# Heads paired as h and h+4, and keys dealt nine tokens to a row

## The chip, the cores and the metric

The kernel runs on one core of a Trainium2 chip. The metric is the device time of one execution in microseconds (us); the kernel before has a median of 513.19 us in three runs (512.69 to 513.75). The core has a matrix engine (TensorE, PE in the profile, with PEld for its weight loads), a vector engine (VectorE, DVE), an activation engine (ScalarE, ACT), a general engine (GpSimd, POOL) and an engine that mostly starts transfers (SyncE, SP). Each takes its instructions in the order in which the program gives them, and they wait for each other by semaphores.

## The reference

```python
q, k, v: (8, 8, 576, 64) float32            # batch, heads, tokens, head_dim
scores = q @ k.T / 8                        # 576 x 576 for each of 64 heads
thresh = max(scores, row) - tau             # tau = 0.02
attn   = softmax(where(scores >= thresh, scores, -1e9))
x      = (attn @ v), heads side by side     # (4608, 512)
h      = x @ w_in                           # (4608, 2048)
g      = h * clip(h + 3, 0, 6) / 6
out    = g @ w_out                          # (4608, 512)
```

The order of the heads in x is free as long as the rows of w_in are taken in the same order, and the order of the keys of a head is free as long as the rows of v are taken in the same order.

## The kernel before

Two heads are a pair, two pairs a quad: 16 quads, two for each of the 8 batches. The heads of a pair lie in partitions 0 to 63 and 64 to 127 of the transposed tiles `qT` and `kT` (head_dim on the partitions, tokens along them), so that two score matmuls work in the two halves of the array. A pair has 4 tiles of 128 query rows and one rest of 64; the rests of both pairs of a quad share a tile. So a quad has 9 slots, and 144 slots n = 0 to 143 follow each other in one written-out loop (`for n, sl in enumerate(queue)`). Everything around it is placed by n: the dictionaries `turns` (transposes of q and k of a later quad), `products` (attention times v), and the lists `loads`, `vcasts`, `casts`, of which `start` takes transfers at the end of a slot. There is no scheduler: the order in the text is the order on each engine.

For slot n, two heads: `scores(n)` (L295, PE), `sm_max` (L310, DVE: copy out of PSUM with the row maximum), `sm_bias` (L317, POOL), `sm_mask` (L322, ACT), `sm_exp` (L327, ACT, with the row sum), `sm_recip` (L330, DVE), `sm_norm` (L335, POOL, writes `pn` in bfloat16). `pn` is transposed by a DMA on SP's queue (L343) or, early on, by PE (L350). `av_main` and `av_rest` (L359, L362) multiply with v; DVE copies the result into `xT` or `xR` (L370, L380).

From slot 22 on (`N1`), each slot also does a piece of the second half: `mm1` (L394 or L389), eight matmuls of x with w_in into PSUM bank `HB`; `mm1_relu` (ACT in even slots, L402; DVE in odd slots, L404); `mm1_gate` (L417, DVE), which frees the bank; and in even slots two parts of `mm2` (L428, 8 matmuls with w_out), copied out every second even slot by DVE (`osb`, L436). Scores are issued by two slots at once at the end of each odd slot. So from about 107 us on, two slots make one round of PE work: L295 (16 matmuls; 24 when one of the slots is the rest of a quad), L394 (even slot), L428, L394 (odd slot), L359 and L362. In such a round DVE does, in this order: copy of `xT`; relu and gate of the odd slot; a transpose of q or k, where `turns` has one; two maxima; gate of the even slot; two maxima; every second round the copy of `osb`.

How q and k get into `qT` and `kT`:

- Batches 0 and 1 (`b < NB`, `by_pe`): loaded in 128 rows, transposed by PE against an identity (L236) and copied out of PSUM. The last 64 tokens of the four heads of a quad come in a tile `kr` (k) and in the end of `nq` (q), as two transfers of 32 KB each (L127), and go through one PE transpose each (L261, L263).
- Batches 2 to 7 (quads 4 to 15): loaded in 32 by 32 blocks, so that VectorE's block transpose from SBUF to SBUF (L245 for q with 576 columns, L251 for k with 512) gives `qT` and `kT` without PE. A pair of q is loaded by four transfers of 72 KB (`blocks_q`), the first 512 keys of a pair by four of 64 KB (`blocks_k`). k is dealt four tokens to a row. The last 64 keys still take the old way: transfers of `kr` (L127; on SP's queue for quad 4, on POOL's from quad 5 on), a PE transpose (L261) in an even slot six or five before the quad, and at the start of the next slot two copies out of PSUM into the two halves of `kT` (`copy_out`, L226, ACT from slot 24 on), columns 576 to 639 for the lower head and 0 to 63 for the upper. `kT` has 640 columns for that reason, and `scores` begins at column 64 for the lower head.

v comes in bfloat16 through POOL's queue (`load_v`, L144 and L147): for batches from 2 on, four transfers for the first 512 tokens, two heads each over 128 partitions, and two for the last 64. w_in comes in 16 transfers of 128 partitions by 512 columns (L165), taken from `casts` in slots 4 to 15, with two in slots 5, 8, 11 and 14.

PSUM has 8 banks. Banks 2 and 5 are handed out in turn by `bank()`, to the PE transposes and to the products with v.

Of the kernel before, what the change touches and what calls it, by code (L numbers as in the profile page):

```python
# [9 lines left out]
F32 = mybir.dt.float32  # L10
# [5 lines left out]
P = 128  # L16
# [4 lines left out]
def kernel(  # L21
# [10 lines left out]
    nc = tc.nc  # L32
# [49 lines left out]

    def load_quad(quad):
        b, g = divmod(quad, 2)
        nat[quad] = (nat_pool.tile([P, 1152], F32, tag="nq", name="nq"),
                     nat_pool.tile([P, 4, 4, D], F32, tag="km", name="km"),
                     nat_pool.tile([P, 2 * D], F32, tag="kr", name="kr"))
        nq, km, kr = nat[quad]

        def main(dst, src, h, order, by=nc.sync):  # L90
            by.dma_start(out=dst[:, :, h, :], in_=src[b, 4 * g + h, 0:512, :].rearrange(order, t=4))

        def blocks_q(n, a, j):
            c = 32 * (2 * a + j)
            nc.sync.dma_start(out=nq[c:c + 32, n * S:(n + 1) * S].rearrange("p (k d) -> p k d", d=32),
                              in_=q[b, 4 * g + 2 * n + a, :, 32 * j:32 * j + 32].rearrange("(k r) d -> r k d", r=32))

        def blocks_k(n, a, j):
            c = 32 * (2 * a + j)
            nc.sync.dma_start(  # L100
                out=km[c:c + 32].rearrange("p t h d -> p (t h d)")[:, n * 512:(n + 1) * 512].rearrange(
                    "p (t m d) -> p t m d", t=4, d=32),
                in_=k[b, 4 * g + 2 * n + a, 0:512, 32 * j:32 * j + 32].rearrange("(m r t) d -> r t m d", r=32, t=4))

        def load_k(n):
            if b < NB:
                for a in range(2):
                    main(km, k, 2 * n + a, "(p t) d -> p t d", by=nc.scalar if quad == n == 0 else nc.sync)
            else:
                for a in range(2):  # L110
                    for j in range(2):
                        blocks_k(n, a, j)

        def load_q(n):
            if b < NB:
                for a in range(2):
                    main(nq[:, 0:1024].rearrange("p (t h d) -> p t h d", h=4, t=4), q, 2 * n + a, "(t p) d -> p t d")
            else:
                for a in range(2):
                    for j in range(2):  # L120
                        blocks_q(n, a, j)

        def rest():
            for dst, src in ((kr[:], k), (nq[:, 1024:1152], q))[0:2 if b < NB else 1]:
                for n in range(2):
                    by = nc.scalar if quad == 0 and src is k else nc.sync if quad < 5 else nc.gpsimd
                    by.dma_start(out=dst[64 * n:64 * n + 64, :].rearrange("p (h d) -> p h d", h=2),  # L127
                                 in_=src[b, 4 * g + 2 * n:4 * g + 2 * n + 2, 512:S, :].rearrange("h p d -> p h d"))

        def both():  # L130
            rest()
            load_k(1)

        if b < NB:
            loads.extend((lambda: load_k(0), lambda: load_q(0), rest, lambda: load_k(1), lambda: load_q(1)))
        else:
            loads.extend((lambda: load_q(0), lambda: load_k(0), lambda: load_q(1), both))

    def load_v(b):
        vm = v_pool.tile([P, H, 4 * D], BF16, tag="vm", name="vm")  # L140
        vr = vrs[b % 2]
        vsb[b] = (vm, vr)
        w = 4 if b < NB else 2
        mains = [lambda h=h: nc.gpsimd.dma_start(  # L144
            out=vm[:, h:h + w, :], in_=v[b, h:h + w, 0:512, :].rearrange("h (p t) d -> p h (t d)", t=4))
            for h in range(0, H, w)]
        rests = [lambda a=a: nc.gpsimd.dma_start(  # L147
            out=vr[a * 64:(a + 1) * 64, a, :, :],
            in_=v[b, :, 512:S, :].rearrange("(hp a) p d -> a p hp d", a=2)[a]) for a in range(2)]
        vcasts.extend(mains + rests if b < NB else mains[0:1] + rests + mains[1:])  # L150


    vrs = []
# [6 lines left out]
    w_out_sb = singles.tile([P, NI, d_model], BF16)  # L160

    def load_weights():
        for n4 in range(4):
            for ki in range(KI):
                casts.append(lambda n4=n4, ki=ki: nc.gpsimd.dma_start(  # L165
                    out=w_in_sb[:, ki, n4 * 512:(n4 + 1) * 512],
                    in_=moe_w_in[ki * P:(ki + 1) * P, n4 * 512:(n4 + 1) * 512]))
        for ni in range(NI):
            casts.append(lambda ni=ni: nc.gpsimd.dma_start(
                out=w_out_sb[:, ni, :], in_=moe_w_out[ni * P:(ni + 1) * P, :]))  # L170
# [39 lines left out]
    def kT_of(pair):  # L210
        return qkT[pair // 2][1][:, pair % 2, :]
# [17 lines left out]
    def by_pe(pair):  # L229
        return pair // NPAIR < NB  # L230
# [16 lines left out]
    def transpose_k(pair):  # L247
        if not by_pe(pair):
            n = pair % 2
            km = nat[pair // 2][1][:].rearrange("p t h d -> p (t h d)")  # L250
            nc.vector.transpose(out=kT_of(pair)[:, 64:576], in_=km[:, n * 512:(n + 1) * 512])  # L251
            return None
        pb = main_pe(nat[pair // 2][1], pair)
        return lambda: copy_out(kT_of(pair)[:, 64:576], pb)

    def transpose_rest(quad, of_k=True, of_q=True):
        pb = bank()
        nq, _, kr = nat[quad]
        of_q = of_q and by_pe(2 * quad)
        if of_k:  # L260
            nc.tensor.transpose(pb[:, 0:P], kr[:], identf[:])  # L261
        if of_q:
            nc.tensor.transpose(pb[:, P:2 * P], nq[:, 1024:1152], identf[:])  # L263

        def evict():
            qT, kT = qkT[quad]
            both = pb.rearrange("p (w n t) -> p w n t", n=2, t=64)
            if of_q:
                nc.vector.tensor_copy(out=qT[:, :, 512:S], in_=both[:, 1])
            if of_k:  # L270
                copy_out(kT[0:64, :, S:S + 64], both[0:64, 0])
                copy_out(kT[64:P, :, 0:64], both[64:P, 0])
        return evict
# [9 lines left out]
    def scores(n):  # L283
        quad, slot = divmod(n, NSLOT)
        w0 = 320 if first(n) else 384
        parts = ((0, w0), (w0, S - w0))
        heads = range(2)
        for group in [((a,), parts) for a in heads] if n in (1, 2) else [(heads, (part,)) for part in parts]:
            for i in range(2 if slot == 8 else 1):
                for a, (k0, w) in [(a, part) for part in group[1] for a in group[0]]:  # L290
                    pair = 2 * quad + (i if slot == 8 else slot // 4)
                    rows = slice(64 * i, 64 * i + 64) if slot == 8 else slice(0, P)
                    q0 = 512 if slot == 8 else slot % 4 * P
                    c0, kc = score_col(n, a) + k0, 64 * (1 - a) + k0
                    nc.tensor.matmul(ps_flat[rows, c0:c0 + w],  # L295
                                     qT_of(pair)[a * 64:(a + 1) * 64, q0:q0 + rows.stop - rows.start],
                                     kT_of(pair)[a * 64:(a + 1) * 64, kc:kc + w], start=True, stop=True)
# [56 lines left out]
    def av(pb, pair, pT, cols):  # L354
        b, hp = divmod(pair, NPAIR)
        vm, vr = vsb[b]
        for c in range(4):
            for a in range(2):
                nc.tensor.matmul(pb[a * 64:(a + 1) * 64, :], vm[:, 2 * hp + a, c * D:(c + 1) * D],  # L359
                                 pT[:, 5 * a + c, cols], start=(c == 0), stop=False)  # L360
        for a in range(2):
            nc.tensor.matmul(pb[a * 64:(a + 1) * 64, :], vr[:, a, hp, :], pT[:, 4, cols], start=False, stop=True)  # L362
# [136 lines left out]
    for quad in range(1, NQUAD):  # L499
        n0 = quad * NSLOT  # L500
        first_odd = n0 - 9 + quad % 2
        for i, (job, of) in enumerate((("q", 2 * quad), ("k", 2 * quad), ("rest", quad),
                                       ("q", 2 * quad + 1), ("k", 2 * quad + 1))):
            turn_at(n0 + ((-5, -5, -4, -2, -1) if quad == 1 else (-6, -5, -4, -2, -1))[i] if quad < 3 else
                    first_odd + (0, 2, 3, 4, 6)[i] if quad > 3 else first_odd + (0, 2, 3, 5, 7)[i], job, of)

# [32 lines left out]
    for n, sl in enumerate(queue):  # L539
# [111 lines left out]
        elif n not in (4, 12, 15, 18, 21) and not 23 < n < 30 and (n < 37 or n % 2 == 0):  # L651
            start(loads, 1)
        if n < 4 or 15 < n < 20 or n > 33:
            start(vcasts, 1 if n < N1 or n % 2 else 0)
        else:
            start(casts, 2 if n in (5, 8, 11, 14) or 21 < n < 28 else 1)
        prev = sl
# [87 lines left out]
```

## Time and profile before

| | |
|---|---|
| three runs, median (us) | 513.19 |
| the profiled execution: first to last instruction (us) | 511.0 |
| what lies around it, by the median of the runs (us) | 2.2 |
| PE, DVE, ACT, POOL busy | 99, 87, 88, 58% |
| granted PE clock | 0.999 |
| L261, transposes of kr by PE | 15, 274 ns |
| L226, copies of the last keys by ACT | 24, 253 ns |
| L245, block transposes 128x576 by DVE | 24, 771 ns |
| L251, block transposes 128x512 by DVE | 24, 704 ns |
| L127, transfers of kr issued by POOL | 22, 632 ns |
| L165, transfers of w_in issued by POOL | 16, 569 ns |

The profile is of one execution, and gives of its own time only the span of 511.0 us; the runs are 1.5 to 2.7 us longer than that, which holds what lies before the first and behind the last instruction. A busy share says how much of the span some instruction of the engine was under way. Matmuls overlap, so the rate at which PE works is read from the distance between the starts of its groups, not from their lengths: a PE transpose is under way for 274 ns, but the next matmul starts 0.11 us after it.

### The profile page before, as it was taken

To read this page: it belongs to the slowest core of one execution; us is meant where nothing else is said; L and a number is where in the kernel's file an instruction comes from. 1 tells how busy PE (TensorE), PEld (TensorE's weight loads), DVE (VectorE), ACT (ScalarE), POOL (GpSimd) and SP (SyncE) were. 2 spreads that over 40 slices of the span, in tenths; PEclk is the share of its full clock that TensorE was granted. 3 is DMA by queue.
4 is the path that set the end of the run, shared out by engine and by line. 5 is a ranking of instruction groups with operands and counts; after the bars stand their busy time and mean duration, and the time that the engine had idled before them with its cause. 6 is when DMAs were issued, how large, how long until landed. Compare 5 with 4: busy or idle time off the path is not lost.

```text
span 511.0 us, 12107 instructions
## 1 busy us (share of the span) xinstructions
PE 503.4 (99%) x4132; PEld 319.8 (63%) x4132; DVE 442.8 (87%) x1127; ACT 450.3 (88%) x977; POOL 298.6 (58%) x539
## 2 busy tenths in 40 slices
PE   8999999999999999999999999999999999999997
PEld 7656566666655666666655666666655666667564
DVE  4788899989999999999999999999999999887251
ACT  4999999999999999999999999999999999987160
POOL 2788879666666756656565656666566755552000
PEclk9999999999999999999999999999999999999999
DMA  6998999989999999999899999999999996563132
GB/s 144 182 172 147 153 143 182 174 157 178 188 160 172 163 174 160 205 162 181 150 158 181 154 163 163 179 169 175 163 178 149 187 177 116 114 111 75 72 57 77
DMA packets 314318, 78.77 MB, mean 154 GB/s; under 512 B 296880, under 2 KB 309424, under 8 KB 314256
## 3 DMA queue, kind: packets, MB, share of 16 engines
q1 hardware_dynamic: 294464, 67.90, 78.0%
q0 software_dynamic: 18304, 9.64, 15.6%
q8 instruction: 32, 0.52, 0.4%
q10 hardware_dynamic: 1488, 0.46, 0.4%
q14 instruction: 30, 0.25, 0.2%
HBM read 36.70 MB, written 9.44 MB: 90 GB/s over the span
## 4 chain that ended last, share of the span: by engine, by line
PE 80%; DVE 4%; ACT 3%; issue 1%; DVEq 0%
PE ps L295 24%; PE ps L428 23%; PE ps L394 20%; PE ps L359 7%; PE ps L389 3%; DVE s L310 1%; PE ps L362 1%; ACT s L327 1%; ACT s L322 1%; DVE g L417 1%; DVE r L404 1%; PE ps L668 1%; ACT r L402 1%; PE ps L350 0%; DVE xT L370 0%
## 5 line engine op out<-in xcount | busy, mean ns | idle before, releaser
L335 POOL TENSOR_SCALAR pn<-s,rinv 128x576 bf16<-128x576 f32 x288 | 210.6, 743 | 19.4 <-issue 4.8
L310 DVE TENSOR_SCALAR_CACHE_REDUCE s<-ps 128x576 f32<-128x576 f32 x288 | 205.0, 748 | 13.4 <-POOL pn L335 5.1
L322 ACT ACTIVATE s<-s,bias 128x576 f32<-128x576 f32 x288 | 205.7, 762 | 3.6 <-POOL bias L317 3.2
L327 ACT ACTIVATE s<-s 128x576 f32<-128x576 f32 x288 | 192.5, 671 | 0.3
L295 PE MATMUL ps<-kT,qT 64*128 64x384 f32 (+7 forms) x1280 | 175.5, 419 | 2.1 <-DVE s L310 2.0
L295 PEld LDWEIGHTS ps<-kT,qT 64*128 64x128 f32 (+1 forms) x1280 | 103.7, 175 | 57.8 <-issue 15.6
L394 PE MATMUL ps<-xT,w_in_sb 128*128 128x256 bf16 x1024 | 131.0, 273 | 0.6 <-DVE g L417 0.5
L428 PE MATMUL ps<-w_out_sb,g 128*128 128x512 bf16 x560 | 130.7, 379 | 0.0
L394 PEld LDWEIGHTS <-w_in_sb 128*128 128x128 bf16 x1024 | 95.6, 98 | 40.3 <-issue 21.0
L317 POOL TENSOR_SCALAR bias<-m 128x2 f32<-128x2 f32 (+1 forms) x147 | 27.5, 187 | 148.4 <-DVE rinv L330 132.1
L417 DVE SCALAR_TENSOR_TENSOR g<-r,ps 128x512 bf16<-128x512 f32 x128 | 87.8, 687 | 13.6 <-ACT r L402 9.1
L428 PEld LDWEIGHTS <-g 128*128 128x128 bf16 x560 | 54.6, 98 | 55.0 <-issue 0.4
L402 ACT ACTIVATE r<-ps,three 128x512 f32<-128x512 f32 x81 | 55.4, 686 | 25.1 <-PE ps L394 20.2
L327 ACT ACTIVATION_READ_ACCUMULATOR s<-s 128x1 f32 x288 | 54.5, 189 | 0.0
L404 DVE TENSOR_SCALAR r<-ps 128x512 f32<-128x512 f32 x63 | 42.9, 681 | 0.0
L359 PE MATMUL ps<-pT,vm 128*64 128x256 bf16 (+1 forms) x480 | 39.1, 285 | 0.0
L359 PEld LDWEIGHTS <-vm 128*64 128x64 bf16 x736 | 27.2, 110 | 16.1 <-issue 14.7
L370 DVE CAST xT<-ps 128x256 bf16<-128x256 f32 (+1 forms) x60 | 26.2, 437 | 10.2 <-PE ps L362 10.2
L436 DVE TENSOR_SCALAR osb<-ps 128x512 f32<-128x512 f32 x31 | 20.8, 672 | 8.4 <-PE ps L428 8.4
L310 DVE DVE_READ_ACCUMULATOR s<-ps 128x1 f32 x288 | 23.9, 83 | 0.0
L330 DVE RECIPROCAL rinv<-rsum 128x2 f32<-128x2 f32 x144 | 23.0, 160 | 0.7 <-ACT s L327 0.6
L144 POOL DMA_DIRECT2D vm<-in_v_dram x28 | 21.4, 766 | 0.1
(60 smaller groups left out, 256.6 us busy)
## 6 DMA issues: line engine op xcount, KB each, us to landing
out_dram<-osb SPq DMA_DIRECT2D x31, 256.0 KB, 2.6
nq<-in_q_dram SPq DMA_DIRECT2D x96, 72.0 KB, 3.4
km<-in_k_dram SPq DMA_DIRECT2D x96, 64.0 KB, 3.2
vm<-in_v_dram POOLq DMA_DIRECT2D x24, 128.0 KB, 3.9
nq<-in_q_dram SPq DMA_DIRECT2D x16, 128.0 KB, 4.9
w_in_sb<-in_moe_w_in_dram POOLq DMA_DIRECT2D x16, 128.0 KB, 3.7
w_out_sb<-in_moe_w_out_dram POOLq DMA_DIRECT2D x16, 128.0 KB, 4.1
pT<-pn SPq DMA_TRANSPOSE x117, 3.8
```

Of the source, the lines that this page charges most:

```text
L295: nc.tensor.matmul(ps_flat[rows, c0:c0 + w], qT_of(pair)[a * 64:(a + 1) * 64, q0:q0 + rows.stop - rows.start], kT_of(pair)[a * 64:(a + 1) ...
L310: nc.vector.tensor_scalar(out=sl.s[:, i, :], in0=ps_flat[:, c0:c0 + S], scalar1=1.0, scalar2=None, op0=Alu.mult, op1=Alu.max, accum_out=sl ...
L317: nc.gpsimd.tensor_scalar(out=sl.bias[:, of], in0=sl.m[:, of], scalar1=-scale, scalar2=tau, op0=Alu.mult, op1=Alu.add)
L322: nc.scalar.activation(out=s, in_=s, func=Act.Prelu, bias=sl.bias[:, i:i + 1], scale=scale, alpha=REJECT)
L327: nc.scalar.activation(out=s, in_=s, func=Act.Exp, accum_out=sl.rsum[:, i:i + 1])
L335: nc.gpsimd.tensor_scalar(out=pn[:, i, :], in0=sl.s[:, i, :], scalar1=sl.rinv[:, i:i + 1], scalar2=1.0, op0=Alu.mult, op1=Alu.mult)
L359: nc.tensor.matmul(pb[a * 64:(a + 1) * 64, :], vm[:, 2 * hp + a, c * D:(c + 1) * D], pT[:, 5 * a + c, cols], start=(c == 0), stop=False)
L394: nc.tensor.matmul(ps[:, hb, n * 256:(n + 1) * 256], w_in_sb[:, ki, (ni + n) * P:(ni + n + 1) * P], xT[b][:, ki, c0:c0 + 256], start=(ki = ...
L402: nc.scalar.activation(out=r, in_=hps, func=Act.Relu, bias=three[:])
L404: nc.vector.tensor_scalar(out=r, in0=hps, scalar1=3.0, scalar2=0.0, op0=Alu.add, op1=Alu.max)
L417: nc.vector.scalar_tensor_tensor(out=out, in0=r, scalar=6.0, in1=hps, op0=Alu.min, op1=Alu.mult)
L428: nc.tensor.matmul(o_ps[0], gbuf[:, ni, mt * P:(mt + 1) * P], w_out_sb[:, ni, :], start=(ni == 0), stop=(ni == NI - 1))
```

## The change

Heads h and h+4 make a pair in place of 2h and 2h+1: pair (g, n) of a batch has heads 2g+n and 4+2g+n. The heads of a quad's two pairs, 2g and 2g+1 below and 4+2g and 5+2g above, now lie next to each other in memory, so one transfer brings both for one half of the partitions (`blocks`): two transfers of 144 KB in place of four of 72 KB (q) or 64 KB (k). For k, rows are dealt nine tokens each in place of four, which takes in all 576 keys. `kr` is no longer loaded for quads 4 to 15, and the turn of their `rest` is left out: no PE transpose and no copies. VectorE transposes 576 columns of k for a pair, by two instructions of 320 and 256 columns, each in runs of 64 columns with steps of 128 between them, on both sides. In `kT` both heads now begin at column 0.

v follows: a head's rows are dealt nine tokens each, in four transfers over 64 partitions with four heads each, and two for the tokens that are left. For batch 2 a transfer is started in each slot from 34 to 39 (before, in odd slots alone). w_in's rows are taken in the new order, in 8 transfers over 64 partitions, four pieces of 512 columns each, in place of 16 over 128 partitions, one piece each; empty places in `casts` keep the rest of the list where it was.

```diff
@@ -82,72 +82,72 @@
 
     def load_quad(quad):
         b, g = divmod(quad, 2)
-        nat[quad] = (nat_pool.tile([P, 1152], F32, tag="nq", name="nq"),
-                     nat_pool.tile([P, 4, 4, D], F32, tag="km", name="km"),
-                     nat_pool.tile([P, 2 * D], F32, tag="kr", name="kr"))
+        nat[quad] = (nat_pool.tile([P, 2 * S], F32, tag="nq", name="nq"),
+                     nat_pool.tile([P, 2 * S], F32, tag="km", name="km"),
+                     nat_pool.tile([P, 2 * D], F32, tag="kr", name="kr") if b < NB else None)
         nq, km, kr = nat[quad]
 
-        def main(dst, src, h, order, by=nc.sync):
-            by.dma_start(out=dst[:, :, h, :], in_=src[b, 4 * g + h, 0:512, :].rearrange(order, t=4))
-
-        def blocks_q(n, a, j):
-            c = 32 * (2 * a + j)
-            nc.sync.dma_start(out=nq[c:c + 32, n * S:(n + 1) * S].rearrange("p (k d) -> p k d", d=32),
-                              in_=q[b, 4 * g + 2 * n + a, :, 32 * j:32 * j + 32].rearrange("(k r) d -> r k d", r=32))
-
-        def blocks_k(n, a, j):
-            c = 32 * (2 * a + j)
-            nc.sync.dma_start(
-                out=km[c:c + 32].rearrange("p t h d -> p (t h d)")[:, n * 512:(n + 1) * 512].rearrange(
-                    "p (t m d) -> p t m d", t=4, d=32),
-                in_=k[b, 4 * g + 2 * n + a, 0:512, 32 * j:32 * j + 32].rearrange("(m r t) d -> r t m d", r=32, t=4))
+        def main(dst, src, n, a, order, by=nc.sync):
+            by.dma_start(out=dst[:, 0:1024].rearrange("p (t h d) -> p t h d", h=4, t=4)[:, :, 2 * n + a, :],
+                         in_=src[b, 4 * a + 2 * g + n, 0:512, :].rearrange(order, t=4))
+
+        def blocks(dst, src, a, order, **sizes):
+            rows = src[b, 4 * a + 2 * g:4 * a + 2 * g + 2].rearrange("n t d -> (n t) d")
+            for j in range(2):
+                c = 32 * (2 * a + j)
+                nc.sync.dma_start(out=dst[c:c + 32].rearrange("p (k d) -> p k d", d=32) if len(sizes) == 1 else
+                                  dst[c:c + 32].rearrange("p (t x d) -> p t x d", d=32, t=9),
+                                  in_=rows[:, 32 * j:32 * j + 32].rearrange(order, **sizes))
 
         def load_k(n):
             if b < NB:
                 for a in range(2):
-                    main(km, k, 2 * n + a, "(p t) d -> p t d", by=nc.scalar if quad == n == 0 else nc.sync)
+                    main(km, k, n, a, "(p t) d -> p t d", by=nc.scalar if quad == n == 0 else nc.sync)
             else:
-                for a in range(2):
-                    for j in range(2):
-                        blocks_k(n, a, j)
+                blocks(km, k, n, "(x r t) d -> r t x d", r=32, t=9)
 
         def load_q(n):
             if b < NB:
                 for a in range(2):
-                    main(nq[:, 0:1024].rearrange("p (t h d) -> p t h d", h=4, t=4), q, 2 * n + a, "(t p) d -> p t d")
+                    main(nq, q, n, a, "(t p) d -> p t d")
             else:
-                for a in range(2):
-                    for j in range(2):
-                        blocks_q(n, a, j)
+                blocks(nq, q, n, "(k r) d -> r k d", r=32)
 
         def rest():
-            for dst, src in ((kr[:], k), (nq[:, 1024:1152], q))[0:2 if b < NB else 1]:
+            for dst, src in ((kr[:], k), (nq[:, 1024:1152], q)):
                 for n in range(2):
-                    by = nc.scalar if quad == 0 and src is k else nc.sync if quad < 5 else nc.gpsimd
+                    by = nc.scalar if quad == 0 and src is k else nc.sync
                     by.dma_start(out=dst[64 * n:64 * n + 64, :].rearrange("p (h d) -> p h d", h=2),
-                                 in_=src[b, 4 * g + 2 * n:4 * g + 2 * n + 2, 512:S, :].rearrange("h p d -> p h d"))
-
-        def both():
-            rest()
-            load_k(1)
+                                 in_=src[b].rearrange("(a n) t d -> n a t d", a=2)[2 * g + n, :, 512:S, :].rearrange(
+                                     "a p d -> p a d"))
 
         if b < NB:
             loads.extend((lambda: load_k(0), lambda: load_q(0), rest, lambda: load_k(1), lambda: load_q(1)))
         else:
-            loads.extend((lambda: load_q(0), lambda: load_k(0), lambda: load_q(1), both))
+            loads.extend((lambda: load_q(0), lambda: load_k(0), lambda: load_q(1), lambda: load_k(1)))
 
     def load_v(b):
         vm = v_pool.tile([P, H, 4 * D], BF16, tag="vm", name="vm")
         vr = vrs[b % 2]
         vsb[b] = (vm, vr)
-        w = 4 if b < NB else 2
-        mains = [lambda h=h: nc.gpsimd.dma_start(
-            out=vm[:, h:h + w, :], in_=v[b, h:h + w, 0:512, :].rearrange("h (p t) d -> p h (t d)", t=4))
-            for h in range(0, H, w)]
-        rests = [lambda a=a: nc.gpsimd.dma_start(
-            out=vr[a * 64:(a + 1) * 64, a, :, :],
-            in_=v[b, :, 512:S, :].rearrange("(hp a) p d -> a p hp d", a=2)[a]) for a in range(2)]
-        vcasts.extend(mains + rests if b < NB else mains[0:1] + rests + mains[1:])
+        if b < NB:
+            mains = [lambda h=h: nc.gpsimd.dma_start(
+                out=vm[:, h:h + 4, :], in_=v[b, h:h + 4, 0:512, :].rearrange("h (p t) d -> p h (t d)", t=4))
+                for h in range(0, H, 4)]
+            rests = [lambda a=a: nc.gpsimd.dma_start(
+                out=vr[a * 64:(a + 1) * 64, a, :, :],
+                in_=v[b, 4 * a:4 * a + 4, 512:S, :].rearrange("h p d -> p h d")) for a in range(2)]
+        else:
+            def tokens(a, first, count):
+                return v[b, 4 * a:4 * a + 4].rearrange("h (p t) d -> p h (t d)", t=9)[
+                    :, :, first * D:(first + count) * D]
+
+            mains = [lambda a=a, u=u, first=first: nc.gpsimd.dma_start(
+                out=vm[64 * u:64 * u + 64, 4 * a:4 * a + 4, :], in_=tokens(a, first, 4))
+                for a, u, first in ((0, 0, 0), (0, 1, 5), (1, 0, 5), (1, 1, 1))]
+            rests = [lambda a=a: nc.gpsimd.dma_start(
+                out=vr[a * 64:(a + 1) * 64, a, :, :], in_=tokens(a, 4 * (1 - a), 1)) for a in range(2)]
+        vcasts.extend(mains + rests)
 
 
     vrs = []
@@ -160,11 +160,13 @@
     w_out_sb = singles.tile([P, NI, d_model], BF16)
 
     def load_weights():
+        rows = moe_w_in.rearrange("(a ki d) f -> a d ki f", a=2, ki=KI)
         for n4 in range(4):
-            for ki in range(KI):
-                casts.append(lambda n4=n4, ki=ki: nc.gpsimd.dma_start(
-                    out=w_in_sb[:, ki, n4 * 512:(n4 + 1) * 512],
-                    in_=moe_w_in[ki * P:(ki + 1) * P, n4 * 512:(n4 + 1) * 512]))
+            for a in range(2):
+                casts.append(lambda n4=n4, a=a: nc.gpsimd.dma_start(
+                    out=w_in_sb[64 * a:64 * a + 64, :, n4 * 512:(n4 + 1) * 512],
+                    in_=rows[a, :, :, n4 * 512:(n4 + 1) * 512]))
+                casts.append(lambda: None)
         for ni in range(NI):
             casts.append(lambda ni=ni: nc.gpsimd.dma_start(
                 out=w_out_sb[:, ni, :], in_=moe_w_out[ni * P:(ni + 1) * P, :]))
@@ -247,16 +249,19 @@
     def transpose_k(pair):
         if not by_pe(pair):
             n = pair % 2
-            km = nat[pair // 2][1][:].rearrange("p t h d -> p (t h d)")
-            nc.vector.transpose(out=kT_of(pair)[:, 64:576], in_=km[:, n * 512:(n + 1) * 512])
+            rows = nat[pair // 2][1][:].rearrange("p (t n w) -> p t n w", t=9, n=2)[:, :, n, :]
+            out = kT_of(pair)
+            for u in range(2):
+                e = 5 - u
+                nc.vector.transpose(out=out[:, 0:640].rearrange("p (c u w) -> p c u w", u=2, w=64)[:, 0:e, u, :],
+                                    in_=rows[:, 5 * u:5 * u + e, :])
             return None
-        pb = main_pe(nat[pair // 2][1], pair)
+        pb = main_pe(nat[pair // 2][1][:, 0:1024].rearrange("p (t h d) -> p t h d", h=4, t=4), pair)
         return lambda: copy_out(kT_of(pair)[:, 64:576], pb)
 
     def transpose_rest(quad, of_k=True, of_q=True):
         pb = bank()
         nq, _, kr = nat[quad]
-        of_q = of_q and by_pe(2 * quad)
         if of_k:
             nc.tensor.transpose(pb[:, 0:P], kr[:], identf[:])
         if of_q:
@@ -291,7 +296,7 @@
                     pair = 2 * quad + (i if slot == 8 else slot // 4)
                     rows = slice(64 * i, 64 * i + 64) if slot == 8 else slice(0, P)
                     q0 = 512 if slot == 8 else slot % 4 * P
-                    c0, kc = score_col(n, a) + k0, 64 * (1 - a) + k0
+                    c0, kc = score_col(n, a) + k0, (64 * (1 - a) if by_pe(pair) else 0) + k0
                     nc.tensor.matmul(ps_flat[rows, c0:c0 + w],
                                      qT_of(pair)[a * 64:(a + 1) * 64, q0:q0 + rows.stop - rows.start],
                                      kT_of(pair)[a * 64:(a + 1) * 64, kc:kc + w], start=True, stop=True)
@@ -356,7 +361,7 @@
         vm, vr = vsb[b]
         for c in range(4):
             for a in range(2):
-                nc.tensor.matmul(pb[a * 64:(a + 1) * 64, :], vm[:, 2 * hp + a, c * D:(c + 1) * D],
+                nc.tensor.matmul(pb[a * 64:(a + 1) * 64, :], vm[:, 4 * a + hp, c * D:(c + 1) * D],
                                  pT[:, 5 * a + c, cols], start=(c == 0), stop=False)
         for a in range(2):
             nc.tensor.matmul(pb[a * 64:(a + 1) * 64, :], vr[:, a, hp, :], pT[:, 4, cols], start=False, stop=True)
@@ -501,6 +506,8 @@
         first_odd = n0 - 9 + quad % 2
         for i, (job, of) in enumerate((("q", 2 * quad), ("k", 2 * quad), ("rest", quad),
                                        ("q", 2 * quad + 1), ("k", 2 * quad + 1))):
+            if job == "rest" and quad // 2 >= NB:
+                continue
             turn_at(n0 + ((-5, -5, -4, -2, -1) if quad == 1 else (-6, -5, -4, -2, -1))[i] if quad < 3 else
                     first_odd + (0, 2, 3, 4, 6)[i] if quad > 3 else first_odd + (0, 2, 3, 5, 7)[i], job, of)
 
@@ -651,7 +658,7 @@
         elif n not in (4, 12, 15, 18, 21) and not 23 < n < 30 and (n < 37 or n % 2 == 0):
             start(loads, 1)
         if n < 4 or 15 < n < 20 or n > 33:
-            start(vcasts, 1 if n < N1 or n % 2 else 0)
+            start(vcasts, 1 if n < 40 or n % 2 else 0)
         else:
             start(casts, 2 if n in (5, 8, 11, 14) or 21 < n < 28 else 1)
         prev = sl
```

## The prediction

> **What bounds the kernel now.** I read the page first (span, shares, chain), then the stretches of 20 us, then PE's order of time in the steady part, and last DVE and ACT in the same stretch. The page:
>
> ```profile
> span 511.0 us, 12107 instructions
> PE 503.4 (99%) x4132; PEld 319.8 (63%) x4132; DVE 442.8 (87%) x1127; ACT 450.3 (88%) x977; POOL 298.6 (58%) x539
> PE 80%; DVE 4%; ACT 3%; issue 1%; DVEq 0%
> L245 DVE STREAM_TRANSPOSE qT<-nq 128x576 f32<-128x576 f32 x24 | 18.5, 771 | 0.0
> L251 DVE STREAM_TRANSPOSE kT<-km 128x512 f32<-128x512 f32 x24 | 16.9, 704 | 0.0
> ```
>
> (The last two are from the groups kept apart by shape.) PE carries 80% of the chain that ends last, and from 107 us to 500 us the stretches show it busy without a gap. A busy PE is no proof, so PE's order of time in one part of the steady state (start, length, line, count):
>
> ```profile
> 302.73 1.89 PE L428 MATMUL ps<-w_out_sb,g 128*128 128x512 bf16 x8
> 304.45 0.27 PE L261 MATMUL ps<-identf,kr 128*128 128x128 f32 x1
> 304.56 1.04 PE L394 MATMUL ps<-xT,w_in_sb 128*128 128x256 bf16 x8
> ...
> 308.27 1.05 PE L394 MATMUL ps<-xT,w_in_sb 128*128 128x256 bf16 x8
> 309.15 1.89 PE L428 MATMUL ps<-w_out_sb,g 128*128 128x512 bf16 x8
> 310.98 1.03 PE L394 MATMUL ps<-xT,w_in_sb 128*128 128x256 bf16 x8
> ...
> 315.64 1.89 PE L428 MATMUL ps<-w_out_sb,g 128*128 128x512 bf16 x8
> 317.36 1.04 PE L394 MATMUL ps<-xT,w_in_sb 128*128 128x256 bf16 x8
> ```
>
> From L428 to the next group PE needs 1.72 us (315.64 to 317.36) where it does not wait. The transpose of kr takes 0.11 us of it (304.45 to 304.56), far less than its length of 0.27. In the round after, 309.15 to 310.98 is 1.83: a wait of 0.11, of which the busy share shows nothing. Why is seen on ACT and DVE there:
>
> ```profile
> 306.18 0.51 ACT L226 COPY kT<-ps 64x128 f32<-64x128 f32 x2
> 309.52 0.69 ACT L402 ACTIVATE r<-ps,three 128x512 f32<-128x512 f32 x1
> 310.24 0.69 DVE L417 SCALAR_TENSOR_TENSOR g<-r,ps 128x512 bf16<-128x512 f32 x1 [0.26 <-ACT r L402]
> ```
>
> The two copies of the last keys put ACT 0.5 us back, so its relu (L402) comes late, DVE's gate (L417) waits 0.26 for it and ends at 310.93, and the bank is free for L394 0.05 later. So PE is bound by its own issue, and any wait on the even slot's gate is lost for good. How near DVE is to making it wait, in the round from 299.70:
>
> ```profile
> 299.88 0.42 DVE L370 CAST xT<-ps 128x256 bf16<-128x256 f32 x1
> 300.21 0.68 DVE L404 TENSOR_SCALAR r<-ps 128x512 f32<-128x512 f32 x1
> 300.93 0.69 DVE L417 SCALAR_TENSOR_TENSOR g<-r,ps 128x512 bf16<-128x512 f32 x1
> 301.54 0.70 DVE L251 STREAM_TRANSPOSE kT<-km 128x512 f32<-128x512 f32 x1
> 302.16 0.72 DVE L310 TENSOR_SCALAR_CACHE_REDUCE s<-ps 128x576 f32<-128x576 f32 x1
> ...
> 303.65 0.69 DVE L417 SCALAR_TENSOR_TENSOR g<-r,ps 128x512 bf16<-128x512 f32 x1
> ```
>
> The k transpose lies ahead of the even gate. That gate ends at 304.34; with 0.05 behind it, L394 could start at 304.39, and without kr's transpose PE is ready at 304.45.
>
> **The change, part by part.** (1) *PE transposes of kr, 12 removed.* The first (96.60) lies in a wait of PE for the gate, so it gives nothing; 11 others at 0.11: **1.21 us gained**.
>
> (2) *ACT copies, 24 removed.* The wait that follows them is 0.10 to 0.11 in the six rounds that start at 131.3, 189.5, 247.8, 306.0, 364.2 and 422.4 (0.60); where the copies fall in a round with two products (from 157.2, 215.4, 273.7, 331.9, 390.1) L428 to the next takes 1.76 in place of 1.73, five times 0.03 (0.15); and at 98.98 they lie on the chain itself, and L428 (101.86) to L394 (103.80) takes 1.94, so 0.21. The other copies delay nothing. Together **0.96 gained**. Next to be late there is the relu, which then waits for L394 itself (0.31 to 0.38 in the rounds without copies).
>
> (3) *DVE's k transposes, 24 of 512 columns become 24 pairs of 320 and 256.* The rows for 512 and 576 columns, 704 and 771 ns, give 1.05 ns a column and 0.17 us fixed: 0.50 and 0.44 us. The next instruction starts 0.08 before a transpose ends (301.54 + 0.70 against 302.16). So from start to start 0.42 + 0.36 = 0.78 in place of 0.62: 0.16 more each. The steps between runs of 64 are not in the trace for this operation; the nearest row is a copy into two runs of 64 with a step (L269, 283 ns) against one into 128 columns in a row (L478, 292 ns): no price. Bounds: below, only the 64 more columns, 0.07. Above, if each of the nine runs cost a start of its own, 9 x (0.067 + 0.087) = 1.39 less 0.62, so 0.77. In between, if the second waits for the first's end, 0.50 + 0.44 less 0.08 less 0.62, so 0.24; for that speaks L224, whose second copy into the same tile begins only when the first has ended (75.65; the copy before it, over all partitions, overlaps by 0.08). I take 0.16, since the transposes use all 128 partitions as those that overlap do.
>
> What it costs PE: room is what is left before the even gate makes L394 wait. In the round above DVE is ready for the gate at 303.57 (0.08 into L330, which starts at 303.49), and the gate could start at 304.45 - 0.05 - 0.69 = 303.71: room 0.14. This holds in 8 rounds, those that follow a copy of osb. In 9 others `xT` starts 0.07 earlier in the round, room 0.20; in 6 rounds with 24 score matmuls L394 is due 0.16 later, so 0.36; the first (94.22) lies where DVE waits 0.13 for ACT anyway. So with an addition K the loss is 8(K-0.14) + 9(K-0.20) + 6(K-0.36), each where positive: at 0.16 it is **0.16 lost**, at 0.24 it is 1.16, at 0.77 it is 12.6. Queued behind the transposes are the two maxima and the gate; for the maxima wait bias, mask and the scores two slots on, which have a round's time; the gate is the one that bites.
>
> The Trainium skill, VectorE: DVE Perf Modes, "The DRAIN you can't avoid", says that the next vector operation does not start until the pipe is empty, which speaks against cutting one transpose in two. The maximum above starts 0.08 before the transpose ends, so the trace disagrees for that neighbour; by the rule K would be 0.24 and the whole sum a gain of 1.3.
>
> (4) *Transfers of q, k and kr.* Per quad SP issues 8 in place of 16 (0.50 and 0.63 us each), POOL two kr fewer (0.63); the bytes are the same, 72 KB landing in 3.4 us, 128 KB in 4.9. They start nine slots (29 us) before their transposes, so landing has to grow by 20 us to be seen. Behind them in SP's queue are the transposes of `pn` (landing 3.8, at most 7.6 us), used four to five slots (13 us and more) after they start. Price 0; without that cover a quad's first transpose would be late by what the landing exceeds.
>
> (5) *v.* Batch 2 needs all six transfers before its first product in slot 43; started in 34 to 39 they have 13 us against 6.6 us at the longest. Later batches b start theirs from slot 18b-9 on, have issued all by 18b+2 and need them at 18b+7, 16 us on. POOL is idle for 35 to 40% there. Price 0.
>
> (6) *w_in.* POOL issues one in place of two in slots 5, 8, 11, 14. Behind the pair of issues at 34.49 (1.11 us) the norm is late, DVE's maximum then waits 0.41 for it, and ACT, which is never idle there, waits 0.12 for the bias; the same 0.13 at 55.15. **Up to 0.25 gained**, 0 at the other end; a transfer of two rows per issue may take POOL longer than 0.57, up to 0.77 as for v. The first use, at 72.8 us, is 18 us behind the last issue.
>
> (7) *Banks 2 and 5* change turns without kr; the products find them free by 3.9 us into the round and start at 5.7. Price 0.
>
> Sum: 1.21 + 0.96 + 0.25 - 0.16 = 2.3 us off the span of 511.0. With the 2.2 us around it, as the median of 513.19 has, that is 510.9 us.
>
> **The rivals.** *A: the second transpose waits for the first.* K 0.24: gain 2.42 - 1.16 = 1.3, so 511.9; somewhat more for semaphores between them, 512.8. For it: the pair of L224. Against it: overlap elsewhere on DVE.
>
> *B, slower: DVE's stepped transposes become the bound.* Place: between the odd gate (L417) and the two maxima. It eats the whole gain at K = 0.31 (17K - 2.92 = 2.42) and is slower by 0.2% (1.03 us) from K = 0.37; at the far bound, 0.77, 12.6 - 2.4 gives +10, 523. For it: no row of a transpose in short runs, and PE cannot make up a wait. Against it: the cost per column is the same in both rows, and L269 shows no price for steps.
>
> *C, same: the gain in PE's order is taken by another wait.* Removing 0.11 in eleven rounds leaves the even gate only 0.06 of spare time in the round shown; another 0.1 on ACT or DVE and L394 waits as before. Gains of (1) gone, 2.3 - 1.2 = 1.1, to nothing: 512.1 to 513.2. Against it: rounds without kr run at 6.39 us, twice and more in a row.
>
> *D, slower: transfers.* Fuller bursts of 144 KB or halves over 64 partitions delay a transpose of `pn`: from a landing of 13 us on, PE waits by the excess, once a quad or more: +1 us and over, 514.5. Against it: the longest landing is 7.6.
>
> The Trainium skill, DMA: Bandwidth & Descriptors, "Rules for kernel authors", advises one transfer over 128 partitions, not two over halves, which speaks against (5) and (6). The same bytes landed in 3.7 us (w_in) far ahead of use, so by the rule, too, the sum would stay.
>
> **How the numbers follow.** A change of 0.2%, 1.03 us, is about what a measurement of this kernel can tell from none. Chances: forecast 0.52 (510.3 to 511.7); A 0.16 (511.7 to 512.8, 0.09 of it faster by over 0.2%); C 0.10 (0.03 faster, 0.07 same); B 0.17; D 0.05. Faster 0.52 + 0.09 + 0.03 = 0.64, same 0.07 + 0.07 = 0.14, slower 0.22. The range holds forecast, A and C nearly whole (0.76) and of B and D the quarter nearest (0.05): up to 514.4, which is K of about 0.38; below, 510.2, where DVE's price is nil (gain 2.42, so 510.8) less the 0.5 us by which the runs shown scatter.
>
> **What would show it.** Right: no L261 after 76 us and no copy of 64x128 by ACT, rounds of 6.39 us (6.55 with 24 score matmuls) where 6.50 and 6.64 stood, two rows of L251's successor near 503 and 436 ns, starting 0.42 apart, and L428 to L394 at 1.72 to 1.75. Wrong: these rows clearly longer than their columns say, gaps of PE on `DVE g L417`, or waits on `km`, `pT` or `vm` transfers.

## The result and the profile after

The changed kernel takes 510.82 us (median of 13 runs) against 513.17 for the kernel before in the same runs: a ratio of 0.9959, 95% interval 0.9951 to 0.9967, so 1.7 to 2.5 us less. One of the 13 runs took 513.05 us, the others 510.72 to 511.33. The forecast was 510.9. Line numbers move by 5 from L295 on: L300 are the scores, L315 the maxima, L399 and L394 the two kinds of `mm1`, L407 its relu on ACT, L422 the gate, L433 `mm2`; VectorE's transposes of k are L256.

The page, with the groups of L256 kept apart by shape as before:

```profile
span 509.0 us, 11876 instructions
PE 501.3 (98%) x4120; PEld 318.0 (62%) x4120; DVE 443.7 (87%) x1151; ACT 444.2 (87%) x953; POOL 279.8 (55%) x509
PE 81%; DVE 5%; ACT 1%; issue 1%; DVEq 0%
L256 DVE STREAM_TRANSPOSE kT<-km 128x320 f32<-128x320 f32 x24 | 12.1, 504 | 0.0
L256 DVE STREAM_TRANSPOSE kT<-km 128x256 f32<-128x256 f32 x24 | 9.6, 402 | 0.0
```

The span is 2.0 us shorter. The busy shares hardly move: DVE works 0.9 us more, ACT 6.1 less and POOL 18.8 less; what POOL saves gave no time, as will be seen. ACT's part in the chain falls from 3 to 1%. PE's order of time in the rounds that answer to those shown before (start, length, line, count):

```profile
301.53 1.89 PE L433 MATMUL ps<-w_out_sb,g 128*128 128x512 bf16 x8
303.25 1.04 PE L399 MATMUL ps<-xT,w_in_sb 128*128 128x256 bf16 x8
...
306.96 1.05 PE L399 MATMUL ps<-xT,w_in_sb 128*128 128x256 bf16 x8
307.84 1.89 PE L433 MATMUL ps<-w_out_sb,g 128*128 128x512 bf16 x8
309.57 1.04 PE L399 MATMUL ps<-xT,w_in_sb 128*128 128x256 bf16 x8
```

From L433 to the next group it is now 1.72 and 1.73 us; before it was 1.72 + 0.11 for the transpose of kr, and 1.83 with the wait. All rounds from 118 to 455 us are like this. ACT in the same stretch:

```profile
304.98 0.67 ACT L332 ACTIVATE s<-s 128x576 f32<-128x576 f32 x1
305.64 0.67 ACT L332 ACTIVATE s<-s 128x576 f32<-128x576 f32 x1
306.31 1.43 ACT L327 ACTIVATE s<-s,bias 128x576 f32<-128x576 f32 x2
308.04 0.69 ACT L407 ACTIVATE r<-ps,three 128x512 f32<-128x512 f32 x1 [0.31 <-PE ps L399]
```

With no copies ahead, ACT is done early and the relu waits 0.31 us for L399, as the prediction said it would. That 0.31 is the room which the copies, 0.51 to 0.54 us, overran. And DVE, with the longer transpose, in a round that follows a copy of `osb` and starts at 182.76:

```profile
182.95 0.41 DVE L375 CAST xT<-ps 128x256 bf16<-128x256 f32 x1
184.00 0.69 DVE L422 SCALAR_TENSOR_TENSOR g<-r,ps 128x512 bf16<-128x512 f32 x1
184.60 0.83 DVE L256 STREAM_TRANSPOSE kT<-km 128x320 f32<-128x320 f32 x2
185.36 0.72 DVE L315 TENSOR_SCALAR_CACHE_REDUCE s<-ps 128x576 f32<-128x576 f32 x1
186.76 0.67 DVE L422 SCALAR_TENSOR_TENSOR g<-r,ps 128x512 bf16<-128x512 f32 x1
```

The row of L256 holds both transposes under the shape of the first. They take 0.83 us together and 0.76 from their start to that of the maximum (184.60 to 185.36). Read to the nanosecond it is 0.754 to 0.757 in all 24 places, where one transpose of before took 0.628: 0.13 more. The even gate starts 4.00 us into the round in place of 3.95 and ends at 4.66, and PE goes on to L399 at 4.75 without a wait.

Where the gain lies is found by cutting the span at score matmuls, which both kernels have in the same number (starts of the groups, us):

| stretch | before | after |
|---|---|---|
| 25th to 201st score matmul | 13.93 to 68.74: 54.81 | 13.90 to 68.71: 54.81 |
| 249th to the last, 1280th | 81.52 to 455.78: 374.26 | 81.49 to 453.67: 372.18 |
| the last score matmul to the end of the span | 55.24 | 55.35 |

So all of the 2.0 us come from 81.5 us on, and none from the first part, where w_in is loaded.

### The profile page after: what moved, and what is told of

It reads as the page before. It is cut to its first block, busy times and chain, and to the rows that moved or that the text cites. A ratio compares the mean times of both kernels' runs of the same rounds, so it can differ in the third digit from the quotient of the medians.

```text
span 509.0 us, 11876 instructions
## 1 busy us (share of the span) xinstructions
PE 501.3 (98%) x4120; PEld 318.0 (62%) x4120; DVE 443.7 (87%) x1151; ACT 444.2 (87%) x953; POOL 279.8 (55%) x509
## 4 chain that ended last, share of the span: by engine, by line
PE 81%; DVE 5%; ACT 1%; issue 1%; DVEq 0%
PE ps L300 25%; PE ps L433 23%; PE ps L399 21%; PE ps L364 7%; PE ps L394 3%; DVE s L315 2%; PE ps L367 1%; DVE g L422 1%; DVE r L409 1%; PE ps L675 1%; ACT s L332 0%; ACT r L407 0%; PE ps L355 0%; DVE xT L375 0%; PE ps L238 0%
## 5 line engine op out<-in xcount | busy, mean ns | idle before, releaser
L315 DVE TENSOR_SCALAR_CACHE_REDUCE s<-ps 128x576 f32<-128x576 f32 x288 | 204.8, 747 | 13.6 <-PE ps L300 7.0
L300 PE MATMUL ps<-kT,qT 64*128 64x384 f32 (+7 forms) x1280 | 175.5, 419 | 2.1 <-DVE s L315 2.0
L300 PEld LDWEIGHTS ps<-kT,qT 64*128 64x128 f32 (+1 forms) x1280 | 103.6, 175 | 58.0 <-issue 16.0
L399 PE MATMUL ps<-xT,w_in_sb 128*128 128x256 bf16 x1024 | 131.0, 273 | 0.6 <-DVE g L422 0.6
L433 PE MATMUL ps<-w_out_sb,g 128*128 128x512 bf16 x560 | 130.7, 379 | 0.0
L399 PEld LDWEIGHTS <-w_in_sb 128*128 128x128 bf16 x1024 | 95.6, 98 | 41.4 <-issue 19.8
L422 DVE SCALAR_TENSOR_TENSOR g<-r,ps 128x512 bf16<-128x512 f32 x128 | 87.6, 685 | 11.4 <-ACT r L407 7.7
L433 PEld LDWEIGHTS <-g 128*128 128x128 bf16 x560 | 54.6, 98 | 54.9 <-issue 0.4
L407 ACT ACTIVATE r<-ps,three 128x512 f32<-128x512 f32 x81 | 55.5, 686 | 29.5 <-PE ps L399 24.7
L364 PE MATMUL ps<-pT,vm 128*64 128x256 bf16 (+1 forms) x480 | 39.1, 285 | 0.0
L364 PEld LDWEIGHTS <-vm 128*64 128x64 bf16 x736 | 27.2, 110 | 16.1 <-issue 15.1
L315 DVE DVE_READ_ACCUMULATOR s<-ps 128x1 f32 x288 | 23.8, 82 | 0.0
L439 ACT ACTIVATE osb<-ps 128x512 f32<-128x512 f32 x4 | 2.4, 597 | 20.9 <-PE ps L433 14.6
```

Source lines behind the costliest of these rows:

```text
L300: nc.tensor.matmul(ps_flat[rows, c0:c0 + w], qT_of(pair)[a * 64:(a + 1) * 64, q0:q0 + rows.stop - rows.start], kT_of(pair)[a * 64:(a + 1) ...
L315: nc.vector.tensor_scalar(out=sl.s[:, i, :], in0=ps_flat[:, c0:c0 + S], scalar1=1.0, scalar2=None, op0=Alu.mult, op1=Alu.max, accum_out=sl ...
L364: nc.tensor.matmul(pb[a * 64:(a + 1) * 64, :], vm[:, 4 * a + hp, c * D:(c + 1) * D], pT[:, 5 * a + c, cols], start=(c == 0), stop=False)
L399: nc.tensor.matmul(ps[:, hb, n * 256:(n + 1) * 256], w_in_sb[:, ki, (ni + n) * P:(ni + n + 1) * P], xT[b][:, ki, c0:c0 + 256], start=(ki = ...
L407: nc.scalar.activation(out=r, in_=hps, func=Act.Relu, bias=three[:])
L422: nc.vector.scalar_tensor_tensor(out=out, in0=r, scalar=6.0, in1=hps, op0=Alu.min, op1=Alu.mult)
```

## The experiments

The theory was the prediction's: PE is bound by its own issue; kr's transposes cost it 0.11 us each; ACT's copies cost it what makes the even gate late; all else is covered. The main rival: the gain comes from the transfers, of which there are half as many. The first four runs share a chip and the runs of the kernel before (513.12 us); the last two likewise (512.87 us).

**The yardstick.** No edit.

> The changed kernel once more, as the yardstick of this group of runs: 0.9959 of the kernel before, some 2.1 to 2.3 us less, and 509.0 us from first to last instruction.

Measured: 511.11 us, ratio 0.9958 (0.9946 to 0.9970), 509.3 us from first to last instruction. The stretch from the 249th score matmul on is 372.20 us; the 0.3 us more lie in the first 14 us. So the stretch compares two kernels more finely than the whole time does, and is used below.

**PE's transposes alone put back.**

```diff
 # quads 4 to 15, where kr's turn was
+    pb = bank()
+    nc.tensor.transpose(pb[:, 0:P], identf[:], identf[:])
```

> The changed kernel with one transpose of the identity by PE put back for each of the quads 4 to 15, at the slot where kr's was, with no transfer and no copy out; its result is not used. Theory (PE bound by its own issue): 11 of the 12 cost 0.11 us each, so 1.2 us more than the changed kernel, and rounds of 6.50 us where they lie. Rival (PE has slack that its busy share hides, and the gain came from ACT or from the transfers): no more than 0.2 us.

Measured: 512.19 us, ratio 0.9981 (0.9972 to 0.9990); the stretch is 373.39 us, 1.19 more than the yardstick's. PE's order of time:

```profile
302.20 1.89 PE L433 MATMUL ps<-w_out_sb,g 128*128 128x512 bf16 x8
303.93 0.27 PE L639 MATMUL ps<-identf 128*128 128x128 f32 x1
304.04 1.04 PE L399 MATMUL ps<-xT,w_in_sb 128*128 128x256 bf16 x8
...
308.63 1.89 PE L433 MATMUL ps<-w_out_sb,g 128*128 128x512 bf16 x8
310.36 1.04 PE L399 MATMUL ps<-xT,w_in_sb 128*128 128x256 bf16 x8
```

An operation that is under way for 0.27 us moves the next one by 0.11, eleven times, and nothing takes it back. In the round after there is no wait (1.73), so the wait of before was not PE's own doing. The rival, that PE has slack which its busy share hides, falls.

**ACT's copies alone put back.**

```diff
 # at the start of the slot after that turn; copy_out copies on ACT there
+    both = pb.rearrange("p (w n t) -> p w n t", n=2, t=64)
+    copy_out(kT[0:64, :, S:S + 64], both[0:64, 0])
+    copy_out(kT[64:P, :, S:S + 64], both[64:P, 0])
```

> The changed kernel with the two copies of 64x128 by ACT put back for each of the quads 4 to 15, at the start of the slot where they were, from the PSUM bank in turn into columns of kT that no matmul reads; their result is not used, and no PE transpose is put back. Theory (a late relu on ACT makes the even gate late, and L399 waits for the bank): 0.96 us more, of which 0.21 near 100 us, and 0.10 in each of the six rounds with 24 score matmuls that follow an even quad's copies. It may be more, since the PE transpose no longer gives DVE 0.11 us in the round before. Rival (ACT's 88% leave it room): no more than 0.2 us.

Measured: 513.22 us, ratio 0.9998 (0.9989 to 1.0006); the stretch is 374.45 us, 2.25 more than the yardstick's. That is more than twice the 0.96 that was expected (the expectation said that it might be more, and why, but gave no size): the copies alone bring back the whole time of the kernel before, without one transpose of kr. PE, ACT and DVE of this kernel (L405 is `mm1`, L439 `mm2`, L413 the relu, L428 the gate):

```profile
309.33 1.89 PE L439 MATMUL ps<-w_out_sb,g 128*128 128x512 bf16 x8
311.27 1.03 PE L405 MATMUL ps<-xT,w_in_sb 128*128 128x256 bf16 x8
```

```profile
306.46 0.52 ACT L228 COPY kT<-ps 64x128 f32<-64x128 f32 x2
307.01 0.68 ACT L338 ACTIVATE s<-s 128x576 f32<-128x576 f32 x1
...
309.81 0.69 ACT L413 ACTIVATE r<-ps,three 128x512 f32<-128x512 f32 x1
```

```profile
310.53 0.69 DVE L428 SCALAR_TENSOR_TENSOR g<-r,ps 128x512 bf16<-128x512 f32 x1 [0.37 <-ACT r L413]
```

The wait is 1.94 - 1.73 = 0.21 us here, where it was 0.10 in the kernel before, since no transpose of 0.11 us stands in the round ahead. The lines of ACT come near it: the copies put the exp behind them back by 0.55 us (306.46 to 307.01), the room is 0.31, and 0.24 are left over; with a round longer by 0.11 the room is 0.42, and 0.13 are left over. Over the run there are 0.21 in six rounds with 24 score matmuls (1.26), 0.14 to 0.15 in the five with two products (0.74), 0.21 near 100 us, and 0.03 in each of three more: 2.3, where the stretches differ by 2.25.

**Both put back.** The two edits above together; the transfers of kr stay away.

> The changed kernel with both put back, PE transposes of the identity and the two copies by ACT that follow each, but not the transfers of kr, and with VectorE's transposes of k as changed. Theory: the two costs add, 2.1 to 2.2 us, which is the whole gain, so the time of the kernel before within 0.3 us. Rival (transfers or v and w_in made the gain): 0.3 us at most, so 2 us below the kernel before.

Measured: 513.30 us, ratio 1.0007 (0.9998 to 1.0015); the stretch is 374.44 us against 374.26 of the kernel before.

```profile
302.87 1.89 PE L439 MATMUL ps<-w_out_sb,g 128*128 128x512 bf16 x8
304.59 0.27 PE L645 MATMUL ps<-identf 128*128 128x128 f32 x1
304.70 1.04 PE L405 MATMUL ps<-xT,w_in_sb 128*128 128x256 bf16 x8
...
309.29 1.89 PE L439 MATMUL ps<-w_out_sb,g 128*128 128x512 bf16 x8
311.12 1.03 PE L405 MATMUL ps<-xT,w_in_sb 128*128 128x256 bf16 x8
```

This is the order of the kernel before, 0.11 and then 1.83. The time is that of before, though this kernel has all the larger transfers of q and k, no transfers of kr, the new ones of v and w_in and 30 transfer issues fewer on POOL (22 of kr, 8 of w_in) besides: to the rival that these made the gain nothing is left, for the stretch is 0.18 us longer than before. Of that, 0.09 is one wait near 115 us, which all kernels with the new pairs have (see the last run), and 0.09 lies in the three rounds with 0.03 more. There it is DVE that comes late, in a round that follows a copy of `osb` and starts at 312.75:

```profile
313.00 0.41 DVE L381 CAST xT<-ps 128x256 bf16<-128x256 f32 x1
...
316.74 0.16 DVE L341 RECIPROCAL rinv<-rsum 128x2 f32<-128x2 f32 x1
316.81 0.66 DVE L428 SCALAR_TENSOR_TENSOR g<-r,ps 128x512 bf16<-128x512 f32 x1
```

DVE begins this round 0.25 us behind PE, where it was 0.19 in the changed kernel (182.95 against 182.76), and goes into the even gate without a pause, 4.06 us into the round in place of 4.00; from `mm2` to the next group PE needs 1.75. So with the longer transposes DVE has less than 0.06 us of room left in such a round.

The forecast that "the two costs add" came out in its total (2.2) but not in its form: 1.19 and 2.25 alone, 2.24 together. The copies set the total, and the transposes run in the wait that they leave.

**w_in in 16 transfers.**

```diff
-    rows = moe_w_in.rearrange("(a ki d) f -> a d ki f", a=2, ki=KI)
     for n4 in range(4):
-        for a in range(2):
-            ...  # 64 partitions, four pieces; an empty place behind each
+        for ki in range(KI):
+            ...  # 128 partitions, one piece
```

> The changed kernel with w_in loaded as before, in 16 transfers over 128 partitions and without the empty places, in the old order of rows: the output is not the reference's, the work is the same. The prediction gave 8 transfers fewer up to 0.25 us; the trace of the changed kernel is 0.04 us ahead at 91 us. Theory by that trace: 0.04 us more than the changed kernel, nothing that the times can show, and the round with the first L433 starting at 91.18 in place of 91.14. Rival (the prediction's term): 0.25 us more, the round starting at 91.4.

Measured: 510.99 us, ratio 0.9959 (0.9945 to 0.9972). The round starts at 91.38, but 0.24 of it is already there at the 25th score matmul (14.14, against 13.90); from there to the 201st (68.95) it takes 54.81 us, as in both other kernels. So the eight transfers fewer gave nothing, and the absolute start, of which the expectation made its test, was a poor one: the first 14 us differ by 0.3 us between executions of one kernel.

**v of batch 2 at its old spacing.**

```diff
-        if n < 4 or 15 < n < 20 or n > 33:
-            start(vcasts, 1 if n < 40 or n % 2 else 0)
+        if n < 4 or 15 < n < 20 or n > 29:
+            start(vcasts, 1 if n < N1 or n % 2 else 0)
```

> The changed kernel with v of batch 2 started in odd slots from 31 to 41, as spaced as in the kernel before, in place of each slot from 34 to 39. In the changed kernel PE waits 0.09 us in the round from 112.05, where DVE's maximum starts 0.36 later than in the same round of before, with transfers of v just before and after. Theory (POOL's issue of v in slots next to each other makes that maximum late): the wait is gone, 0.09 us less. Rival (another cause, or chance of one execution): the wait stays.

Measured: 510.84 us, ratio 0.9959 (0.9946 to 0.9971). DVE's maximum in the round that starts at 112.03:

```profile
113.20 0.69 DVE L422 SCALAR_TENSOR_TENSOR g<-r,ps 128x512 bf16<-128x512 f32 x1
114.72 0.76 DVE L315 TENSOR_SCALAR_CACHE_REDUCE s<-ps 128x576 f32<-128x576 f32 x1 [0.83 <-PE ps L300]
116.16 0.67 DVE L422 SCALAR_TENSOR_TENSOR g<-r,ps 128x512 bf16<-128x512 f32 x1
```

It still starts 2.69 us into the round, and L433 to L399 is still 1.82. The wait of 0.09 us is in all six kernels with the new pairs and not in the kernel before, so it is no chance, but v's spacing is not its cause. Nor does the trace show another: when the maximum starts at 114.72, its score matmuls have ended at 114.24 and POOL's last norm at 113.48. The cause stays open.

Not tried on the chip: longer transposes of k, in four or nine instructions, to find where PE begins to wait; one transpose of 576 columns; and smaller transfers of q and k with kr's put back. So DVE's room of 0.14 to 0.36 us is tried only at one length: 0.13 fits, and the runs with ACT's copies show that little is left in the rounds that follow `osb`.

## Why the prediction was right

(1) *PE transposes, 1.21 us.* Measured 1.19 by the kernel that has them alone. The reading from start to start (0.11) in place of the length (0.27) was right; by the length it would have been 3.0. The first one, in a wait, gave nothing, as said.

(2) *ACT's copies, 0.96 us.* From the kernel before to the one that keeps PE's transposes but not the copies the stretch shrinks from 374.26 to 373.39, 0.87, with the 0.09 of the round at 112 us against it: 0.96. Between the two runs that differ by the copies alone (both put back, and PE's transposes put back) it is 1.05, with the 0.09 of DVE's three rounds. The sum (1) + (2) holds, since both were removed, and in the order copies, then transposes. What the prediction did not see is that the two are not two separate prices: without the copies' removal that of the transposes would have gained nothing, as the run with the copies alone shows. Rival C had the form of it, a wait on ACT or DVE that takes up what PE's order gains. With the copies left in, it would have come true.

(3) *VectorE's transposes, 0.16 us lost.* Measured 0.13 more from start to start in place of 0.16, and no loss, as the prediction's own formula gives for 0.13. The steps cost nothing that shows: the first of the two has the length that the straight line gave (504 ns), the second is shorter (402 against 436). The second also starts before the first has ended: two instructions of 504 and 402 take 0.83 us. So rival A does not hold for this pair; its 0.24 did not appear. The prediction took the rule of the Trainium skill (VectorE: DVE Perf Modes, "The DRAIN you can't avoid") without its exception: the section says, too, that a next operation which is not held starts earlier, as this pair does.

(4) and (5) *Transfers of q, k, kr and v, no price.* Those of 144 KB land in 4.4 us (q) and 3.9 us (k), where 72 and 64 KB took 3.4 and 3.2; v's 128 KB land in 4.0 over 64 partitions, where it was 3.9 over 128; `pn`'s transposes in 4.0 in place of 3.8. No wait of PE or DVE names a transfer in the steady part. The advice of the Trainium skill against two transfers to halves of the partitions (DMA: Bandwidth & Descriptors, "Rules for kernel authors") was not put to the test: w_in's transfers of 256 KB over 64 partitions land in 5.2 us, where 128 KB over 128 took 3.7, and no engine waits for them.

(6) *w_in, up to 0.25 us gained.* Wrong: nothing. The step that failed is the chain from the two issues on POOL to a late norm and from there to the wait of the maximum. Norm and maximum before, then in the changed kernel:

```profile
35.95 1.47 POOL L335 TENSOR_SCALAR pn<-s,rinv 128x576 bf16<-128x576 f32 x2
37.06 0.76 DVE L310 TENSOR_SCALAR_CACHE_REDUCE s<-ps 128x576 f32<-128x576 f32 x1 [0.41 <-POOL pn L335]
```

```profile
35.72 1.47 POOL L340 TENSOR_SCALAR pn<-s,rinv 128x576 bf16<-128x576 f32 x2
37.03 0.76 DVE L315 TENSOR_SCALAR_CACHE_REDUCE s<-ps 128x576 f32<-128x576 f32 x1 [0.42 <-issue]
```

With one issue fewer the norm starts 0.23 us earlier, and the maximum waits as long as before; it starts 1.35 us behind the start of its score matmuls before (35.71) and 1.36 in the changed kernel (35.67). ACT's two waits for the bias, 0.12 and 0.13 before, are 0.13 each. The wait was put down to POOL before (0.41) because POOL's signal came last among those that are shown, not because it was what the maximum waited for; what that was is not shown. The prediction gave 0 as the other end of this term.

(7) *Banks 2 and 5, no price.* No wait on the products is seen (the page has 0.0 us of idle time before L364); the 0.09 near 115 us is not explained, so this is not excluded there.

The sum of 2.3 was 2.08 in the steady part and 2.0 in the span: 0.25 of w_in missing, 0.16 for DVE not paid, 0.09 lost in one round, and 0.11 in the tail. That the forecast of 510.9 lies within 0.1 us of the median is in part luck: two terms were wrong in opposite directions, and the medians differ by 2.35 us where the two profiled spans differ by 2.0. The profiled execution of the kernel before was one of its quicker ones: later runs of it with a span of 511.0 us took 512.75 to 512.82, against a median of 513.17.

## What to carry to other kernels

Where an engine is bound by issue, price a removed instruction by how far it moves the next one, and look behind it for waits that the busy share hides. Two removals in the same rounds may share one wait: ask of each what it gives if the other stays, and look for the engine with room in one part of a round that it overruns in another. A releaser named in a trace is a candidate; compare the start with the work that feeds it before a gain is built on it.

## What was not expected of the hardware

A block transpose on VectorE that followed another was shorter than the straight line through the others says: 402 ns for 256 columns, where 504 ns for 320, 704 for 512 and 771 for 576 lie on one line that gives 436. No run has 256 columns by themselves, so whether the place or the size does it is not shown. And the first 14 us of one and the same kernel differ by 0.3 us between two executions, while the 372.2 us of its steady part agree within 0.02.
